# Banded attention into a feed-forward network: attention of two tiles at a time, the first block's cells partly in halves

## The chip, the cores and the metric

One core of one Trainium2 chip. The metric is the device time of one execution, in microseconds (us). Before the change the median of three runs is 890.47 us (890.44 to 892.8).

## What is computed

```python
# attention: 8 batches, 8 heads, 576 tokens, 64 values per head
scores = scale * np.matmul(q, k.transpose(0, 1, 3, 2))
mask = (rel >= 0) & (rel < 64)              # rel: query position minus key position
attn = softmax(np.where(mask, scores, -1e9))
x = heads_side_by_side(np.matmul(attn, v))   # 4608 tokens x 512
# network: w_in 512 x 2048, w_out 2048 x 512, alpha per hidden unit
h = x @ w_in
g = np.maximum(h, 0.0) + alpha * np.minimum(h, 0.0)
return (g @ w_out).astype(np.float32)
```

All is in 32-bit floats; the network's weights arrive as 64-bit floats and are converted on the core.

## The kernel before

Each matmul of the network is made of three: operands are split into a high and a low part (`xh`, `xl`, `wh`, `wl`), and high x high, high x low and low x high are added up.

**Attention** works on 36 tiles of 128 tokens, all eight heads of a tile together (`attention`, line 466). A tile's steps are: load q, k and v (SyncE's DMA queue); scores (`score`, line 404, TensorE, 32 matmuls of 64 x 64 weights into two banks of PSUM); masked minimum per head (`take_least`, 413, VectorE); exponential per head (`exponential`, 420, ScalarE); reciprocals of the sums (`invert`, 425 and 426, VectorE); scaling (`scale`, 430, GpSimd); turning the weights, either by VectorE's 16 transposes (440 and 442, the 23 tiles in `TURNED`) or by eight TensorE transposes (447) and copies out of PSUM (451); values (`value`, 463, TensorE, 48 matmuls); split into `xh` and `xl` (504 and 506).

**The first product** runs over 9 blocks of 4 tiles (512 tokens). A block has 16 cells (`cell`, line 513): 128 hidden units by 512 tokens, 12 matmuls (522) into one of four banks, then ScalarE's scaled copy (527), VectorE's max (528) and a store to memory, by way of four buffers. A cell of block n needs all four tiles of that block. Attention of block n + 1 stands between the cells of block n; that of tiles 0 to 3 comes ahead of the first cell. Tiles share one buffer of turned weights (`pt`).

**Weights** come in chunks (`chunk`, 302): ScalarE (318, 319), VectorE (323 or 321, 325), GpSimd (327), then the split (292, 288 or 289). The 16 chunks of `w_in` are converted while block 0 runs, those of `w_out` in blocks 1, 2, 4 and 5.

**The second product** (`second`, 561) follows, 36 units of seven steps of 12 matmuls (610), and is the same before and after.

**The order** is made by a planner (`Program.order`, line 73): each operation has an engine or a choice of two, a duration written into the program, the buffers that it reads and writes, and for TensorE a due time (`key`). The planner plays the engines, takes the ready operation that is due first, and writes down the order; each engine of the chip then runs its own list in that order, and waits for the others' results. From `ident` on until the fourth cell (`order`, line 662) gaps in TensorE's list are filled with dummy matmuls (`warm`, 274).

Of the kernel before, what the change touches and what calls it, by code (L numbers as in the profile page):

```python
# [41 lines left out]
class Op:  # L42
    def __init__(self, name, ways, key, earliest, service, at):
        self.name, self.ways, self.key, self.earliest, self.service, self.at = name, ways, key, earliest, service, at
        self.engine = next(iter(ways)) if len(ways) == 1 else None
        self.done = min(busy + LAGS[e] for e, (busy, _) in ways.items()) + (service + LANDING if "SP" in ways else 0.0)
        self.after, self.then, self.needs, self.due, self.begun = set(), [], 0, 0.0, False


class Program:  # L50
# [6 lines left out]
    def add(self, name, ways, reads=(), writes=(), key=None, earliest=0.0, service=0.0):  # L57
        o = Op(name, ways, key, earliest, service, len(self.ops))
# [14 lines left out]
    def order(self, fill):  # L73
# [7 lines left out]
        events, order, lanes, line, now = [], [], [], 0.0, 0.0  # L81
# [40 lines left out]
        while left:  # L122
            for e in ENGINES:
# [15 lines left out]
                o.busy = o.ways[e][0]  # L139
                order.append((now, o))  # L140
# [32 lines left out]
def banded_attention_then_prelu_ffn(  # L173
# [55 lines left out]
    turned = work.tile([P, 2, 2, 2, 2, W], F32, name="pt")  # L229
# [4 lines left out]
    ulps = work.tile([P, 512], I32, name="ulps")  # L234
# [4 lines left out]
    H_BANK, S_BANK, V_BANK = (0, 1, 2, 3), (4, 5), (6, 7)  # L239
# [33 lines left out]
    def warm():  # L273
        nc.tensor.matmul(banks[H_BANK[3]][:, :P], ident, ident, start=True, stop=True)  # L274
# [12 lines left out]
    def subtract_of(out, a, b):  # L287
        return {"DVE": (0.64, lambda: nc.vector.tensor_tensor(out=out, in0=a, in1=b, op=ALU.subtract)),
                "POOL": (1.29, lambda: nc.gpsimd.tensor_tensor(out=out, in0=a, in1=b, op=ALU.subtract))}

    def split(name, value, reads, hi, lo, hi_key, lo_key, earliest=0.0):
        p.add(name + ".h", {"ACT": (0.6, lambda: nc.scalar.copy(hi, value)), "POOL": (0.65, lambda: nc.gpsimd.tensor_copy(hi, value))},  # L292
              reads, [hi_key], earliest=earliest)
        p.add(name + ".l", subtract_of(lo, value, hi.bitcast(F32)), [*reads, hi_key], [lo_key], earliest=earliest)

    def two(name, to, a, b, op, reads, writes, earliest=0.0):
        p.add(name, {"DVE": (0.64, lambda: nc.vector.tensor_tensor(out=to, in0=a, in1=b, op=op)),
                     "POOL": (1.29, lambda: nc.gpsimd.tensor_tensor(out=to, in0=a, in1=b, op=op))}, reads, writes, earliest=earliest)
# [3 lines left out]
    def chunk(name, c, f, second, start=0.0):  # L302
        r = raw_at[0] % len(raws)
        raw_at[0] += 1
# [13 lines left out]
        add("rd." + name, "ACT", 0.57, lambda: nc.scalar.activation(ulps, low, AF.Copy, scale=2.0**-29), [k_raw], keys("e.ulps"), earliest=start)  # L318
# [3 lines left out]
        else:  # L322
            sh = lambda: nc.vector.tensor_scalar(out=bits, in0=bits, scalar1=3, scalar2=None, op0=ALU.logical_shift_left)  # L323
        add("sh." + name, "DVE", 0.6, sh, ["signs"] if second else [], [k_val], earliest=start)
        add("sg." + name, "DVE", 0.62, lambda: nc.vector.scalar_tensor_tensor(  # L325
            out=bits, in0=high, scalar=-2**31, in1=bits, op0=ALU.bitwise_and, op1=ALU.bitwise_xor), [k_raw], [k_val], earliest=start)
        p.add("jn." + name, {"POOL": (1.29, lambda: nc.gpsimd.tensor_tensor(out=bits, in0=bits, in1=ulps, op=ALU.add)),  # L327
                             "DVE": (0.66, lambda: nc.vector.tensor_tensor(out=bits, in0=bits, in1=ulps, op=ALU.add))},
              ["e.ulps"], [k_val, *both], earliest=start)
# [66 lines left out]
    def score(t):  # L396
        q = queries[t % 2].rearrange("p a (h w) -> p a h w", h=2)
        at = 2 * (t % KRING)
        for a in range(2):
            for h in range(2):  # L400
                for u in range(2):
                    for x in range(2):
                        r, us = slice(x * D, (x + 1) * D), slice(u * W, (u + 1) * W)
                        nc.tensor.matmul(bank_of(S_BANK[x])[us, 2 * a + h], q[r, a, h, us], kring[r, a, at + u:at + u + 2, h, :],  # L404
# [5 lines left out]
    def take_least(t, g):  # L410
# [3 lines left out]
            out=of_head(weights[t % 2], g), in0=bank_of(S_BANK[x])[:, e].rearrange("p (b k) -> p b k", b=2),  # L414
# [7 lines left out]
    def invert(t, u):  # L422
# [287 lines left out]
```

## Time and profile before

| | |
|---|---|
| profiled execution, its own time | 889.79 us |
| its span, first to last instruction | 888.1 us |
| TensorE (PE) busy | 872.5 us, 98%, 7910 matmuls |
| VectorE (DVE) busy | 698.0 us, 79% |
| ScalarE (ACT) busy | 458.7 us, 52% |
| GpSimd (POOL) busy | 205.0 us, 23% |
| granted clock of TensorE, mean | 0.998 |
| DMA, mean | 172 GB/s |
| chain that ended last, TensorE's share | 93% |

A busy share is a mean over stages with different limits, and TensorE's dummy matmuls count as busy. Matmuls overlap, so the length of one row is more than the time until the next starts; where the text counts TensorE's time it goes by the distance from start to start.

### The profile page before, as it was taken

The numbers are of one execution on the slowest core, as the hardware profiler recorded it, in microseconds if no ns is written. First come the engines' busy times: TensorE is split into PE (matmuls) and PEld (weight loads), VectorE is DVE, ScalarE is ACT, GpSimd is POOL, SyncE is SP. The second block draws the span as 40 slices with busy tenths as digits, with TensorE's granted clock in tenths as the row PEclk, the third lists the DMA queues.
The fourth block names the chain that finished last, engine by engine and source line by source line (L and its number), as shares of the span: only waits on it lengthen the run. The fifth ranks groups of instructions, "written<-read, shape, count | busy, mean of one in ns | idle before, by whom it ended". The sixth has DMA issues, their size and how long they took to land.

```text
span 888.1 us, 21316 instructions
## 1 busy us (share of the span) xinstructions
PE 872.5 (98%) x7910; PEld 781.7 (88%) x7910; DVE 698.0 (79%) x1835; ACT 458.7 (52%) x1176; POOL 205.0 (23%) x186
## 2 busy tenths in 40 slices
PE   7998899999999999999999999999999999999998
PEld 7986687888888888888888899999999999999997
DVE  3789889887797889779587457878888787878772
ACT  5887766565365674654553344444444444444440
POOL 4796645382017445311110000000000000000000
PEclk9999999999999999999999999999999999999999
DMA  6768654665366884744535995534444443535201
GB/s 188 237 206 257 196 170 158 214 198 184 114 199 232 270 270 161 260 156 138 179 114 178 354 323 178 159 108 150 119 140 131 136 143 108 154 107 156 72 25 48
DMA packets 121207, 152.91 MB, mean 172 GB/s; under 512 B 10512, under 2 KB 92432, under 8 KB 121104
## 3 DMA queue, kind: packets, MB, share of 16 engines
q1 hardware_dynamic: 121104, 151.56, 54.0%
q8 instruction: 62, 1.02, 0.5%
q14 instruction: 41, 0.34, 0.1%
HBM read 95.95 MB, written 55.57 MB: 171 GB/s over the span
## 4 chain that ended last, share of the span: by engine, by line
PE 93%; DVE 4%; issue 1%; POOL 1%; ACT 1%; POOLq 0%
PE bank L522 41%; PE bank L610 41%; PE bank L463 4%; PE bank L404 4%; PE bank L274 3%; PE bank L447 1%; DVE val L325 1%; DVE pt L440 1%; DVE val L323 1%; DVE pt L442 1%; ACT w L420 1%; DVE cell L528 1%; POOL w L430 0%; POOL val L327 0%; DVE xl L506 0%
## 5 line engine op out<-in xcount | busy, mean ns | idle before, releaser
L582 ACT CAST xh<-g 128x512 fp32r<-128x512 f32 x216 | 132.8, 621 | 155.0 <-PE bank L610 128.4
L583 DVE TENSOR_TENSOR xl<-g,xh 128x512 fp32r<-128x512 f32 x216 | 147.7, 689 | 38.5 <-ACT xh L582 35.1
L527 ACT ACTIVATE cell<-bank,alphas 128x512 f32<-128x512 f32 x144 | 98.9, 687 | 141.1 <-PE bank L522 132.8
L522 PE MATMUL bank<-xh,wh 128*128 128x512 f32 x576 | 161.4, 402 | 1.9 <-ACT wh L292 1.9
L610 PE MATMUL bank<-wh,xh 128*128 128x256 f32 x1008 | 161.3, 282 | 0.0
L610 PE MATMUL bank<-wl,xh 128*128 128x256 f32 x1008 | 161.3, 282 | 0.0
L610 PE MATMUL bank<-wh,xl 128*128 128x256 f32 x1008 | 161.3, 282 | 0.0
L522 PE MATMUL bank<-xl,wh 128*128 128x512 f32 x576 | 154.5, 390 | 0.0
L522 PE MATMUL bank<-xh,wl 128*128 128x512 f32 x576 | 154.1, 389 | 0.0
L528 DVE SCALAR_TENSOR_TENSOR cell<-bank,alphas,cell 128x512 f32<-128x512 f32 x144 | 105.2, 745 | 56.7 <-ACT cell L527 49.5
L610 PEld LDWEIGHTS bank<-wh,xh 128*128 128x128 f32 x1008 | 138.6, 191 | 0.1
L610 PEld LDWEIGHTS bank<-wl,xh 128*128 128x128 f32 x1008 | 138.2, 191 | 0.0
L610 PEld LDWEIGHTS bank<-wh,xl 128*128 128x128 f32 x1008 | 138.2, 191 | 0.0
L522 PEld LDWEIGHTS bank<-xl,wh 128*128 128x128 f32 x576 | 108.2, 188 | 23.5
L522 PEld LDWEIGHTS bank<-xh,wl 128*128 128x128 f32 x576 | 108.1, 188 | 22.8
L522 PEld LDWEIGHTS bank<-xh,wh 128*128 128x128 f32 x576 | 104.4, 189 | 26.4 <-issue 3.1
L420 ACT ACTIVATE w<-w,nm 128x128 f32<-128x128 f32 x288 | 111.9, 392 | 28.6 <-DVE nm L413 28.5
L430 POOL TENSOR_TENSOR w<-w,rc 128x512 f32<-128x512 f32 x72 | 78.2, 1087 | 185.9 <-DVE rc L426 174.6
L440 DVE STREAM_TRANSPOSE pt<-w 32x256 f32<-32x256 f32 x184 | 80.1, 436 | 5.7 <-POOL w L430 3.2
L578 DVE TENSOR_TENSOR g<-g,g 128x512 f32<-128x512 f32 x108 | 74.3, 688 | 2.1 <-DMA g<-g 0.6
L413 DVE CUSTOM_DVE_ANT_0 w<-bank,masks 128x128 f32<-128x128 f32 x288 | 63.9, 285 | 12.7 <-PE bank L404 11.2
L442 DVE STREAM_TRANSPOSE pt<-w 32x128 f32<-32x128 f32 x184 | 55.7, 303 | 2.9
(58 smaller groups left out, 763.8 us busy)
## 6 DMA issues: line engine op xcount, KB each, us to landing
g<-cell SPq DMA_DIRECT2D x144, 256.0 KB, 3.9
g<-g SPq DMA_DIRECT2D x144, 256.0 KB, 3.4
q<-qT SPq DMA_DIRECT2D x36, 256.0 KB, 4.3
out<-cell SPq DMA_DIRECT2D x36, 256.0 KB, 2.3
raw<-w_in SPq DMA_DIRECT2D x16, 512.0 KB, 4.7
raw<-w_out SPq DMA_DIRECT2D x16, 512.0 KB, 5.3
k<-kT SPq DMA_DIRECT2D x18, 384.0 KB, 4.2
v<-vN SPq DMA_DIRECT2D x18, 384.0 KB, 4.0
```

Of the source, the lines that this page charges most:

```text
L413: nc.vector.tensor_tensor_reduce(out=of_head(weights[t % 2], g), in0=bank_of(S_BANK[x])[:, e].rearrange("p (b k) -> p b k", b=2), in1=mask ...
L420: nc.scalar.activation(w, w, AF.Exp, scale=-1.0, bias=least[t % 2][:, g:g + 1], accum_out=sums[:, t % 2, g, 0:1])
L430: nc.gpsimd.tensor_tensor(out=w, in0=w, in1=rc.unsqueeze(1).unsqueeze(3).broadcast_to(list(w.shape)), op=ALU.mult)
L440: nc.vector.transpose(to, w[:, x, j])
L442: nc.vector.transpose(to[:, :, j ^ 1], w[:, x, j, :, j ^ 1])
L522: nc.tensor.matmul(h, w[KEPT + f][:, a * P:(a + 1) * P], v[:, a], start=k == a == 0, stop=k == 2 and a == NP - 1)
L527: add(f"sl.{n}.{f}", "ACT", 0.7, lambda: nc.scalar.activation(g, h, AF.Copy, scale=slope[:, f:f + 1]), ["signs", f"bank.{bank}"], [f"cell. ...
L528: add(f"la.{n}.{f}", "DVE", 0.72, lambda: nc.vector.scalar_tensor_tensor(out=g, in0=h, scalar=sign[:, f:f + 1], in1=g, op0=ALU.mult, op1=A ...
L578: add(name, "DVE", 0.64, lambda: nc.vector.tensor_tensor(out=to(), in0=a(), in1=b(), op=op), reads, writes)
L582: add(f"ys.{u}.{i}.h", "ACT", 0.6, lambda: nc.scalar.copy(x_hi[x], value()), ks, [f"xh.{x}"])
L583: add(f"ys.{u}.{i}.l", "DVE", 0.64, lambda: nc.vector.tensor_tensor(out=x_lo[x], in0=value(), in1=x_hi[x].bitcast(F32), op=ALU.subtract), ...
L610: nc.tensor.matmul(banks[bank][:, h * EH:(h + 1) * EH], part[x][:, j * HW + h * P:j * HW + (h + 1) * P], w[k][:, j * EH:(j + 1) * EH], sta ...
```

## The change

- Tiles 0 to 3 go one by one as before (`attend_one`), turned by TensorE in the banks of the scores. From tile 4 on two tiles go together (`attend_two`): one TensorE operation computes the scores of two tiles, and right behind it another the values of the two tiles before, so a stretch is scores, scores, values, values. The scores wait until the tiles before are ready for their values. Each tile of a pair has its own two banks of scores and its own buffer of turned weights.
- The cells get two banks in place of four.
- Each transpose of VectorE is an operation of its own for the planner (before, four were one). TensorE turns tiles 0 to 7, 9, 14, 19, 24, 29 and 34; VectorE the other 22.
- From tile 4 on all eight reciprocals of a tile are one operation. The splits into `xh` and `xl` take two tiles at a time.
- In block 0 the first five cells are computed in two halves of 256 tokens, the first half as soon as tiles 0 and 1 are there; the second halves stand between the whole cells 5 to 15.
- The fill of dummy matmuls ends with the second half cell (`h.0.1.0`).
- The low bits of the weights (`ulps`) get two buffers. Loads of v are issued behind the values before.
- The planner's durations and due times are others, and it plays GpSimd's operations and VectorE's ones with two inputs from SBUF (`paired`) one after the other.

The core of the diff:

```diff
-BEGIN = 30.0
-CELL = 3.22
+BEGIN = 16.0
+CELL = 3.25
 UNIT = 10.1
 STEP = 1.44
-TURNED = tuple(t for t in range(6, 36) if t % 4)
+SINGLE = 4
+HALVES = (18.0, 32.0)
+EARLY_HALVES = 5
+PACE = 3.8
+FIRST_TURNS = (34.0, 52.0, 68.0)
+PE_TURNED = (4, 5, 6, 7, *range(9, 36, 5))
...
                 o.busy = o.ways[e][0]
+                if e == "POOL" and o.busy or e == "DVE" and o.paired:
+                    o.busy += max(0.0, shared - now)
+                    shared = now + o.busy
...
-    turned = work.tile([P, 2, 2, 2, 2, W], F32, name="pt")
+    turned = [work.tile([P, 2, 2, 2, 2, W], F32, name=f"pt_{i}") for i in range(2)]
...
-    ulps = work.tile([P, 512], I32, name="ulps")
+    ulp_ring = [work.tile([P, 512], I32, name=f"ulps_{i}") for i in range(2)]
...
-    H_BANK, S_BANK, V_BANK = (0, 1, 2, 3), (4, 5), (6, 7)
+    H_BANK, S_BANK, V_BANK = (0, 1), ((2, 3), (4, 5)), (6, 7)
...
-        nc.tensor.matmul(banks[H_BANK[3]][:, :P], ident, ident, start=True, stop=True)
+        nc.tensor.matmul(banks[H_BANK[1]][:, :P], ident, ident, start=True, stop=True)
...
-    def transpose(t, u, i):
-        w = weights[t % 2]
+    def transpose(t, u, i, x, j):
+        pt = turned[t % 2]
         r = slice(u * W + i * 32, u * W + i * 32 + 32)
-        w = w[r].rearrange("p a b (h x) (j k) -> p x j a b h k", x=2, j=2)
-        for x in range(2):
-            for j in range(2):
-                to = turned[x * W + j * 32:x * W + j * 32 + 32, :, :, u, :, i * 32:i * 32 + 32].rearrange("p a h b q -> p a b h q")
-                if i == j:
-                    nc.vector.transpose(to, w[:, x, j])
-                else:
-                    nc.vector.transpose(to[:, :, j ^ 1], w[:, x, j, :, j ^ 1])
...
+    def turn(t, u, to):
         for b in range(2):
             for h in range(2):
-                nc.tensor.transpose(bank_of(V_BANK[u])[:, 2 * b + h],
+                nc.tensor.transpose(bank_of(to[u])[:, 2 * b + h],
...
+        for us in ([0], [1]) if t < SINGLE else ([0, 1],):
+            heads = slice(us[0] * NP, (us[-1] + 1) * NP)
+            add(f"rc.{t}.{us[0]}", "DVE", 0.3, lambda heads=heads: invert(t, heads), [f"e.sum.{t % 2}.{g}" for g in range(NH)[heads]], keys(*(f"e.rc.{t % 2}.{u}" for u in us)))
...
+        if not by_pe:
             for u in range(2):
                 for r in range(2):
-                    add(f"tr.{t}.{u}.{r}", "DVE", 1.4, lambda u=u, r=r: transpose(t, u, r), [f"{w}{g}" for g in range(NH)], keys(f"e.pt.{u}.{r}"))
-        else:
-            for u in range(2):
-                heads = range(u * NP, (u + 1) * NP)
-                add(f"tu.{t}.{u}", "PE", 0.44, lambda u=u: turn(t, u), [*(f"{w}{g}" for g in heads), "ident"], [v_banks[u]], key=begin + 0.5 * pace)
-                p.add(f"td.{t}.{u}", {"ACT": (0.57, lambda u=u: take_turned(t, u, nc.scalar.copy)), "DVE": (0.6, lambda u=u: take_turned(t, u, nc.vector.tensor_copy))},
-                      [v_banks[u]], keys(f"e.pt.{u}.0", f"e.pt.{u}.1"))
-        add(f"av.{t}", "PE", 0.95, lambda: value(t), [*vs, *(f"e.pt.{u}.{i}" for u in range(2) for i in range(2))], v_banks, key=begin + pace)
+                    for x in range(2):
+                        for j in range(2):
+                            add(f"tr.{t}.{u}.{r}.{x}.{j}", "DVE", 0.45 if r == j else 0.315, lambda u=u, r=r, x=x, j=j: transpose(t, u, r, x, j), w,
+                                keys(f"e.pt.{t % 2}.{u}.{r}.{x}.{j}"))
+
+    def turned_by_pe(t, to, key):
+        for u in range(2):
+            add(f"tu.{t}.{u}", "PE", 0.44, lambda u=u: turn(t, u, to), [*w_keys(t, u), "ident"], [f"bank.{to[u]}"], key=key)
+            p.add(f"td.{t}.{u}", {"ACT": (0.5, lambda u=u: take_turned(t, u, to, nc.scalar.copy)), "DVE": (0.6, lambda u=u: take_turned(t, u, to, nc.vector.tensor_copy))},
+                  [f"bank.{to[u]}"], keys(*pt_keys(t, [u])))
...
+    def x_parts(ts):
+        n, i = divmod(ts[0], BT)
...
+            from_ = bank_of(V_BANK[x]).rearrange("p (a i) q -> p a (i q)", a=2)[:, :, :len(ts) * P]
...
+    def attend_one(t, begin, pace):
+        loads(t, 0.0)
+        ring_load("v", t, 0.0)
+        add(f"s.{t}", "PE", 1.0, lambda: score(t), [f"e.q.{t % 2}", *ring_keys("k", t)], s_banks(t), key=begin)
+        softmax(t, True)
+        turned_by_pe(t, S_BANK[t % 2], begin + 0.5 * pace)
+        add(f"av.{t}", "PE", 1.0, lambda: value(t, 0), [*ring_keys("v", t), *pt_keys(t)], v_banks, key=begin + pace)
+        x_parts([t])
...
+    def values_of(ts, key):
+        def emit():
+            for i, t in enumerate(ts):
+                value(t, i)
+
+        add(f"av.{ts[0]}", "PE", 2.0, emit, [*(k for t in ts for k in ring_keys("v", t)), *(k for t in ts for k in pt_keys(t))], v_banks, key=key)
+        x_parts(ts)
+
+    def attend_two(ts, begin, before):
+
+        by_pe = [t for t in before if t in PE_TURNED]
+        for t in by_pe:
+            turned_by_pe(t, V_BANK, begin - 0.02)
+        if ts:
+            for t in ts:
+                loads(t, max(0.0, begin - 35.0))
+
+            def emit():
+                for t in ts:
+                    score(t)
+
+            wait = [k for t in before for k in (w_keys(t) if t in by_pe else pt_keys(t))]
+            add(f"s.{ts[0]}", "PE", 2.0, emit, [*(f"e.q.{t % 2}" for t in ts), *(k for t in ts for k in ring_keys("k", t)), *wait],
+                [k for t in ts for k in s_banks(t)], key=begin)
+        if before:
+            values_of(before, begin + 0.01)
+        for t in ts:
+            ring_load("v", t, max(0.0, begin - 20.0))
+        for t in ts:
+            softmax(t, t in PE_TURNED)
...
+    def cell(n, f, key, m=None):
...
+        at = counted[0] + (counted[0] % 2 if m is None else 0)
+        counted[0] = at + (2 if m is None else 1)
+        bank, c = H_BANK[at // 2 % 2], at // 2 % len(cells)
+        d, j, x = f % 8 // 2, f % 2, f // 8
+        parts = [0, 1] if m is None else [at % 2]
+        half = slice(0, 2 * HW) if m is None else slice(m * HW, (m + 1) * HW)
+        to = slice(parts[0] * HW, (parts[-1] + 1) * HW)
+        h, g = banks[bank][:, to], cells[c][:, to]
...
+                    nc.tensor.matmul(h, w[KEPT + f][:, a * P:(a + 1) * P], v[:, a, half], start=k == a == 0, stop=k == 2 and a == NP - 1, skip_group_check=True)
...
+        add(f"h.{name}", "PE", 12 * (0.2267 if m is None else 0.12), emit, [f"wh.{KEPT + f}", f"wl.{KEPT + f}", *needs], k_h, key=key)
+        add(f"sl.{name}", "ACT", 0.1 + 0.52 * part, lambda: nc.scalar.activation(g, h, AF.Copy, scale=slope[:, f:f + 1]), ["signs", *k_h], k_g)
...
-    for t in range(BT):
-        attention(t, 8.0 + 4.5 * t, 5.0)
+    for t in range(SINGLE):
+        attend_one(t, 6.0 + 4.5 * t, 5.0)
     for f in range(NF):
         convert_in(f)
+    pair = lambda j: [t for t in (2 * j, 2 * j + 1) if t < NT]
+    attend_two(pair(SINGLE // 2), FIRST_TURNS[0], [])
     for n in range(NB):
-        if n + 1 < NB:
-            for i in range(BT):
-                attention((n + 1) * BT + i, begin_of(n) + (i - 0.7) * 4 * CELL, 4 * CELL)
+        turns = [(2 * n + 3, 4), (2 * n + 4, 12)]
+        for j, f in turns:
+            if pair(j - 1):
+                attend_two(pair(j), begin_of(n) + (f - 0.5) * CELL if n else FIRST_TURNS[j - 2], pair(j - 1))
         for f in range(NF):
-            cell(n, f)
+            if n:
+                cell(n, f, begin_of(n) + f * CELL)
+        if n == 0:
+            for f in range(EARLY_HALVES):
+                cell(n, f, HALVES[0] + f * PACE, 0)
+            for f in range(NF - EARLY_HALVES):
+                if f < EARLY_HALVES:
+                    cell(n, f, HALVES[1] + f * PACE, 1)
+                cell(n, EARLY_HALVES + f, HALVES[1] + (f + 0.5) * PACE)
...
-    order = p.order(("ident", "h.0.3"))
+    order = p.order(("ident", "h.0.1.0"))
```

## Rows read from the trace of the kernel before

**Rows 1.** Windows: length, busy us (instructions) PE, PEld, DVE, ACT, POOL; clock, DMA, GB/s.
```profile
0.00:43.00 43.00, 38.36 (x629) 35.83 (x630) 23.03 (x138) 29.84 (x113) 24.26 (x32) 1.00 0.70 209
43.00:107.00 64.00, 57.39 (x500) 45.64 (x499) 55.66 (x163) 48.56 (x138) 47.26 (x39) 0.97 0.72 230
107.00:523.00 416.00, 416.00 (x3761) 339.64 (x3759) 329.98 (x1090) 225.04 (x674) 133.51 (x116) 1.00 0.61 199
```

**Rows 2.** The chain that ended last, in time: start, length, what.
```profile
523.16 360.65 PE bank L610 x3024
```

**Rows 3.** TensorE's timeline, first block's ends: start, length, engine, line, operation, count.
```profile
43.08 1.18 PE L522 MATMUL bank<-xh,wh 128*128 128x512 f32 x4
...
105.88 1.07 PE L522 MATMUL bank<-xh,wl 128*128 128x512 f32 x4
```

**Rows 4.** TensorE's waits: total, times, longest.
```profile
PE bank L463 <- DVE pt L440: 4.3, 2, 3.9
```

**Rows 5.** TensorE's timeline around stretches of attention.
```profile
124.48 1.13 PE L463 MATMUL bank<-pt,v 64*64 64x128 f32 x48
125.44 1.05 PE L404 MATMUL bank<-k,q 64*64 64x128 f32 x32
126.42 1.20 PE L522 MATMUL bank<-xh,wh 128*128 128x512 f32 x4
...
129.27 1.07 PE L522 MATMUL bank<-xh,wh 128*128 128x512 f32 x4
...
131.99 1.07 PE L522 MATMUL bank<-xh,wh 128*128 128x512 f32 x4
...
137.52 1.10 PE L404 MATMUL bank<-k,q 64*64 64x128 f32 x32
...
159.81 1.03 PE L447 MATMUL bank<-ident,w 128*128 128x128 f32 x8
160.59 1.17 PE L522 MATMUL bank<-xh,wh 128*128 128x512 f32 x4
...
245.34 1.10 PE L404 MATMUL bank<-k,q 64*64 64x128 f32 x32
246.26 1.08 PE L463 MATMUL bank<-pt,v 64*64 64x128 f32 x48
```

**Rows 6.** VectorE's timeline where tile 1's low parts are written.
```profile
26.62 0.75 DVE L506 TENSOR_TENSOR xl<-bank,xh 128x256 fp32r<-128x256 f32 x2
```

**Rows 7.** ScalarE's groups, 8 to 107 us: busy, mean ns, idle before.
```profile
L420 ACT ACTIVATE w<-w,nm 128x128 f32<-128x128 f32 x80 | 31.2, 395 | 10.0 <-DVE nm L413 10.0
```

**Rows 8.** VectorE's groups, 8 to 107 us.
```profile
L440 DVE STREAM_TRANSPOSE pt<-w 32x256 f32<-32x256 f32 x16 | 7.0, 435 | 0.6 <-POOL w L430 0.4
...
L442 DVE STREAM_TRANSPOSE pt<-w 32x128 f32<-32x128 f32 x16 | 4.8, 303 | 0.3
```

**Rows 9.** TensorE's and VectorE's timeline in the last block.
```profile
509.40 1.07 PE L522 MATMUL bank<-xh,wh 128*128 128x512 f32 x4
...
510.32 0.75 DVE L528 SCALAR_TENSOR_TENSOR cell<-bank,alphas,cell 128x512 f32<-128x512 f32 x1 [1.97 <-ACT cell L527]
```

**Rows 10.** The same two in the second block.
```profile
170.14 1.07 PE L522 MATMUL bank<-xh,wh 128*128 128x512 f32 x4
...
174.91 1.40 DVE L528 SCALAR_TENSOR_TENSOR cell<-bank,alphas,cell 128x512 f32<-128x512 f32 x2
```

**Rows 11.** The page's DMA issues: count, KB each, median us to landing.
```profile
k<-kT SPq DMA_DIRECT2D x18, 384.0 KB, 4.2
```

**Rows 12.** TensorE's timeline at its longest wait.
```profile
92.97 0.43 PE L463 MATMUL bank<-pt,v 64*64 64x128 f32 x2 [3.93 <-DVE pt L440]
93.76 1.98 PE L463 MATMUL bank<-pt,v 64*64 64x128 f32 x46 [0.36 <-DVE pt L440]
95.67 1.87 PE L522 MATMUL bank<-xh,wh 128*128 128x512 f32 x4
```

**Rows 13.** Windows, one stretch behind that wait.
```profile
95.00:96.00 1.00, 1.00 (x23) 0.88 (x16) 0.97 (x8) 0.25 (x2) 0.75 (x1) 0.50 0.00 0
```

More of the change, by code (lines that the diff above doesn't have):

```diff
@@ L80, in order @@
         until = dict.fromkeys(ENGINES, 0.0)
-        events, order, lanes, line, now = [], [], [], 0.0, 0.0
+        events, order, lanes, line, shared, now = [], [], [], 0.0, 0.0, 0.0
         left, filling = len(ops), False
@@ new lines, in ring_load, with loads, w_keys @@
+    def ring_load(kind, t, early):
+        new = slice(0 if t % KRING == 0 else 1, 3)
+        load = load_k if kind == "k" else load_v
+        add(f"{kind}.{t}", "SP", 0.5, lambda: load(t), (), keys(*ring_keys(kind, t)[new]), service=1.35 if t % KRING == 0 else 0.95, earliest=early)
+    def loads(t, early):
+        add(f"q.{t}", "SP", 0.5, lambda: load_q(t), (), keys(f"e.q.{t % 2}"), service=0.9, earliest=early)
+        ring_load("k", t, early)
+    def w_keys(t, u=None):
+        return [f"e.w.{t % 2}.{g}" for g in (range(NH) if u is None else range(u * NP, (u + 1) * NP))]
@@ L510, in begin_of @@
     def begin_of(n):
         return BEGIN + n * CELL * NF
-    def cell(n, f):
-        at = n * NF + f
-        bank, c, d, j, x = H_BANK[at % 4], at % 4, f % 8 // 2, f % 2, f // 8
-        h, g = banks[bank], cells[c]
+    counted = [0]
+    def cell(n, f, key, m=None):
[7 more added lines that the diff above has]
+        h, g = banks[bank][:, to], cells[c][:, to]
+        k_h, k_g = [f"bank.{bank}.{i}" for i in parts], [f"cell.{c}.{i}" for i in parts]
@@ L517, in cell @@
         xh, xl = xs[n % 2]
+        part = 1.0 if m is None else 0.5
         def emit():
@@ L521, in emit @@
                 for a in range(NP):
-                    nc.tensor.matmul(h, w[KEPT + f][:, a * P:(a + 1) * P], v[:, a], start=k == a == 0, stop=k == 2 and a == NP - 1)
-        slots = [4 * (n % 2) + a for a in range(NP)]
-        add(f"h.{n}.{f}", "PE", 12 * 0.2267, emit, [f"wh.{KEPT + f}", f"wl.{KEPT + f}", *(f"{part}.{i}" for i in slots for part in ("xh", "xl"))],
-            [f"bank.{bank}"], key=begin_of(n) + f * CELL)
-        add(f"sl.{n}.{f}", "ACT", 0.7, lambda: nc.scalar.activation(g, h, AF.Copy, scale=slope[:, f:f + 1]), ["signs", f"bank.{bank}"], [f"cell.{c}.0"])
@@ new lines, in cell @@
+        add(f"la.{name}", "DVE", 0.06 + 0.6 * part, lambda: nc.vector.scalar_tensor_tensor(
+            out=g, in0=h, scalar=sign[:, f:f + 1], in1=g, op0=ALU.mult, op1=ALU.max), ["signs", *k_h], k_g)
+        far_to = hidden[n][d].rearrange("p (m x) j t -> p x j m t", x=2)[:, x, j]
+        if m is None:
+            store = lambda: nc.sync.dma_start(far_to, g.rearrange("p (m t) -> p m t", m=2))
+        else:
+            store = lambda: nc.sync.dma_start(far_to[:, m], g)
+        add(f"gs.{name}", "SP", 0.5, store, k_g, [f"far.g.{n}.{d}.{2 * y + x}.{j}" for y in (range(2) if m is None else [m])], service=0.9 * part)
```

142 lines of the change are left out of this document (69 added, 73 removed).

## The prediction

> **What bounds the kernel now.** I read the busy table by stage first, then TensorE's waits, then TensorE's timeline where they fall. The windows [rows 1] cut the run at the first cell of the first product (43 us), the end of its first block of tokens (107 us) and the start of the second product (523 us). From 107 to 523 us TensorE is busy in 416.00 of 416 us; after that the chain of waits runs through one unbroken piece of 3024 matmuls, 360.65 us [rows 2]. There only less TensorE work can save time. Before 107 us a busy TensorE misleads: most of it up to 43.08 us, where the first cell starts [rows 3], is attention of four tiles and dummy matmuls of the fill. Between 43 and 107 us it stands still for 6.6 us, and the longest wait is 3.9 us for the transposes of VectorE [rows 4]. So there are two places to gain: what TensorE spends beside its cells after 107 us, and how late the first block ends. That is at 105.88 + 0.91 = 106.8 us, where the last four matmuls of its last cell end [rows 3].
>
> The sum is made against the profiled execution, 889.8 us (span 888.1 and 1.7 around it). The median of the runs shown, 890.47, lies 0.7 above; my number is on the scale of the profiled one, and the range covers that.
>
> **Pairs, after the first block.** A cell is 131.99 - 129.27 = 2.72 us. From 126.42 to 137.52 lie four cells, 11.10 us, 0.22 more than 4 x 2.72: that is what a stretch of small matmuls costs the cells at its two edges. A stretch "values then scores" takes 126.42 - 124.48 = 1.94, so 2.16 with its edges [rows 5]. From 106.8 to 523.0 us, 128 cells make 348.2 of 416.2 us, and attention has 68.0. Counted in the timeline, these are 17 stretches of two pieces (36.7 us), 20 of one piece, and six tiles turned by TensorE at 160.59 - 159.81 = 0.78 and some 0.1 at the edges (5.3). The 20 lone pieces are left with 26.0, 1.30 each, edges included.
> The change needs for the same 26 scores and 28 values 13 stretches of four pieces and a last one of two values. Values ahead of scores take 125.44 - 124.48 = 0.96, scores ahead of values 246.26 - 245.34 = 0.92, scores ahead of a cell 0.98 [rows 5]. Scores ahead of scores are in no row; I take 0.92, its nearest neighbour, with 0.85 to 0.98 as ends. One stretch: 0.92 + 0.92 + 0.96 + 0.98 + 0.22 = 4.0 us. 13 x 4.0 + 2.2 + 5.3 (again six turned tiles) = 59.5. The gain is 68.0 - 59.5 = 8.5; I take 8, between 7 and 9.5.
>
> **The first block.** TensorE's own list until its end, in the changed order: 16 cells 43.5; five of them as halves cost 24 x 360.65 / 3024 = 2.86 instead of 2.72 each [rows 2], +0.7; four single tiles, each 2 x 1.30 + 0.9, 14.0; scores of tiles 4 and 5, 2.2; two stretches of four, 8.0; tiles 4 to 7 turned, 3.6. Sum 72.0. A half cell needs tiles 0 and 1 alone; VectorE wrote the low part of tile 1 at 26.62 to 27.4 us [rows 6], so that is when it could start. Ahead of it TensorE has three scores, two values and two turned tiles, 8.3 of the 27.4 us: 19.1 are lost to the chain of the softmax. With no other wait the block ends at 72.0 + 19.1 = 91 us.
> The helpers hardly allow that. ScalarE was busy 29.84 + 48.56 = 78.4 us up to 107 [rows 1]; 16 of its 80 exponentials (0.39 us each, 6.3 in all [rows 7]) belong to tiles 8 and 9, which the next block needs; two more tiles turned by TensorE add four copies out of PSUM and the halves five more reads, about +3, an estimate that takes them as eight instructions of 0.39. That is 75 us from about 10 us on: 85 at no idle time, 93 at a tenth idle, against a fifth now. VectorE loses the transposes of tiles 6 and 7, 7.0 + 4.8 = 11.8 us [rows 8], which stood in front of the longest wait; they go to TensorE. I put the end at 95: the 91, and 4 for weights that come late. The gain is 106.8 - 95 = 11.8. Its ends are 16 (no such wait) and 4 (end at 103, if the conversion sets the pace as now).
>
> **Two banks for the cells in place of four.** This is the wait that the change adds. Undisturbed, a cell's bank is free 1.67 us after its end: the cell ends at 509.40, VectorE's max runs from 510.32 to 511.07 [rows 9]. With two banks the cell after the next starts 2.72 us after that end, so 1.0 us may be lost to whatever ScalarE and VectorE have in hand. With four banks nobody had to hurry: the cell that ends at 170.14 is read by a max that begins at 174.91, behind sixteen transposes [rows 10]. The plan now must cut in, and can, since each transpose is an operation of its own, of 0.30 to 0.44 us [rows 8]. A late max holds all cells and the next stretch behind it on TensorE, and the loss is paid in full. I take 3 us in all, 0.02 per cell; ends 0 and 9.
>
> **Nothing for the rest.** Loads of k and q may now wait for the stretch before: some 25 us (eight cells and a stretch) ahead of their use against 4.2 us of landing [rows 11]; without that cover a stretch would start 4 us late. On SyncE's queue they stand ahead of stores of cells, and four cell buffers cover some 11 us. One load for two tiles' values and merged casts save VectorE and ScalarE tenths, off the path. The second buffers for turned weights and low bits only loosen waits. The planner's new durations and its shared turn of GpSimd and VectorE move the order alone, and their worth is in the waits above. The second product is the same instructions in the same order and stays at its length.
>
> **The sum.** 889.8 - 8 - 11.8 + 3 = 873.0 us.
>
> **Rivals.**
> - *A, nothing waits:* the first block ends at 91 and two banks cost nothing: 889.8 - 8 - 16 = 866. For it: TensorE has not one wait in 416 us now [rows 1], from a plan with coarser times. Against it: ScalarE would need almost no idle time.
> - *B, the first block is paced by the helpers:* it ends at 103 as weights and softmax come no sooner. 889.8 - 8 - 4 + 3 = 881. For it: VectorE is busy 55.66 of 64 us between 43 and 107 us [rows 1]. Against it: 11.8 us of that go.
> - *C, the clock:* after its wait of 3.93 us TensorE runs at a granted clock of 0.50, its 1.2 GHz level, and the piece from 93.76 to 95.67 lasts 1.91 instead of about 1.0, the next four matmuls are slow as well: some 1.6 us lost [rows 12, 13]. The fill of dummy matmuls that covered all gaps up to 43 us now ends with the second half cell, near 28 us, so later gaps are bare. Three such gaps cost 4.8: 873 + 5 = 878. It speaks against this that the waits summed above are 4 us in all, in pieces.
> - *D, two banks decide, and the kernel gets slower:* if the max ends late by a mean of 0.2 us per cell, 144 cells lose 28.8: 889.8 - 8 - 11.8 + 28.8 = 899. It decides from 19.8 / 144 = 0.14 us per cell. For it: VectorE is 79% busy from 107 to 523 us and works in long runs [rows 1, 10]. Against it: a queue that is planned for it needs to place one max every 2.72 us, and a transpose in hand costs 0.44 of the 1.0 us.
>
> On C, the Trainium skill ("TensorE: Matmul & The Clock Gate", Part 1) says that the slow clock is the default state and that only activity releases it, which speaks against a shorter fill. By that rule the sum would be the 878 of C instead of 873. The trace agrees for its one long wait (0.50 [rows 13]).
>
> **Chances.** The forecast 0.48, A 0.16, B 0.16, C 0.10, D 0.10. The predicted time is the forecast's, 873. The range 863 to 884 holds A, B and C with a few us of spread (the ends of the pairs and of the waits) and leaves out D and the tails. A measurement of this kernel can tell about 0.3%, 2.7 us. Faster by more than that: the forecast, A, C and nearly all of B, 0.88; within it: the rest of B and a mild D, 0.04; slower: D, 0.08.
>
> **What would show it.** Right: 15 stretches of 64 score and 96 value matmuls, about 3.8 us each, no TensorE idle between them and the second product 416 - 5 = 411 us after the end of the first block; first cells with 256 columns near 27 us; the first block's end near 95 us. Wrong: waits of first product matmuls for VectorE's cell (D, every one on the bank); waits for ScalarE's or GpSimd's weights between 40 and 100 us and an end past 100 (B); a granted clock of 0.50 in windows before 95 us (C); a stretch that waits for transposes, which would be a new wait that I priced at nothing.

## The result and the profile after

The changed kernel takes 879.89 us (median of four runs, 878.87 to 883.31) against 890.72; the ratio is 0.988, with an interval of 0.9849 to 0.9911. The forecast was 873.0, its range 863 to 884. The profiled execution took 878.87 us, 10.9 less than the one before. The three stretches of [rows 1], cut in the changed kernel where they now end: first cell, end of the first block, start of the second product (length, then busy us and instructions of PE, PEld, DVE, ACT, POOL; clock, DMA share, GB/s).

```profile
0.00:27.00 27.00, 22.37 (x342) 20.91 (x343) 14.30 (x80) 17.33 (x66) 12.61 (x22) 1.00 0.72 202
27.00:101.00 74.00, 66.69 (x791) 57.96 (x790) 57.21 (x185) 64.09 (x190) 54.72 (x46) 0.98 0.79 246
101.00:512.00 411.00, 407.75 (x3757) 341.26 (x3756) 331.05 (x1037) 213.15 (x627) 134.60 (x119) 1.00 0.62 203
```

After the first block TensorE is no longer busy all the time: 407.75 of 411 us. The events that cut these stretches, from TensorE's timeline (start, length, what, and idle time ahead in brackets) and, last, from the chain of waits:

```profile
27.03 0.71 PE L599 MATMUL bank<-xh,wh 128*128 128x256 f32 x4
...
100.58 1.07 PE L599 MATMUL bank<-xh,wh 128*128 128x512 f32 x4
...
512.52 0.64 PE L691 MATMUL bank<-wh,xh 128*128 128x256 f32 x4
...
512.68 360.65 PE bank L691 x3024
```

The first half cell starts at 27.03 (forecast 27.4, before 43.08 [rows 3]). The first block ends at 100.58, where the next block's first cell begins (forecast 95, before 106.8). From there to the second product it is 512.52 - 100.58 = 411.9 us (forecast 411, before 416.2). What follows lasts 877.2 - 512.5 = 364.7 us, before 888.1 - 523.0 = 365.1. So 6.2 + 4.3 + 0.4 = 10.9 us came from these three places.

TensorE's waits in the changed kernel (total, times, longest), to be laid beside [rows 4]:

```profile
PE bank L599 <- DVE cell L606: 4.9, 4, 2.6
PE bank L282 <- POOL ident L266: 4.6, 1, 4.6
PE bank L599 <- ACT wh L300: 1.7, 1, 1.7
PE bank L469 <- issue: 1.2, 2, 0.7
PE bank L469 <- ACT pt L457: 1.1, 1, 1.1
PE bank L599 <- POOL wl L297: 0.9, 1, 0.9
PE bank L453 <- POOL w L438: 0.8, 1, 0.8
```

The long wait for transposes is gone. In its place stands the wait that the change added: a cell of the first product that may not enter its bank until VectorE's max (L606) has read it.

### The profile page after: what moved, and what is told of

Read it like the earlier page. It is cut to its first block, busy times and chain, and to the rows that moved or that the text cites. A ratio compares the mean times of both kernels' runs of the same rounds, so it can differ in the third digit from the quotient of the medians.

```text
span 877.2 us, 21173 instructions
## 1 busy us (share of the span) xinstructions
PE 858.1 (98%) x7912; PEld 781.1 (89%) x7912; DVE 690.9 (79%) x1745; ACT 449.9 (51%) x1135; POOL 201.9 (23%) x185
## 4 chain that ended last, share of the span: by engine, by line
PE 88%; DVE 4%; ACT 3%; DMA 2%; issue 1%; POOL 1%; POOLq 0%; DVEq 0%; SPq 0%; ACTq 0%
PE bank L691 41%; PE bank L599 39%; PE bank L469 3%; PE bank L413 3%; DMA raw<-w_in 2%; ACT w L429 2%; DVE cell L606 1%; PE bank L282 1%; PE bank L453 1%; DVE pt L446 1%; DVE val L334 1%; DVE pt L448 0%; ACT val L328 0%; DVE val L332 0%; POOL val L306 0%
## 5 line engine op out<-in xcount | busy, mean ns | idle before, releaser
L605 ACT ACTIVATE cell<-bank,alphas 128x512 f32<-128x512 f32 (+1 forms) x149 | 100.2, 673 | 168.2 <-PE bank L599 155.1
L599 PE MATMUL bank<-xh,wh 128*128 128x512 f32 (+1 forms) x596 | 159.0, 388 | 6.6 <-DVE cell L606 4.9
L606 DVE SCALAR_TENSOR_TENSOR cell<-bank,alphas,cell 128x512 f32<-128x512 f32 (+1 forms) x149 | 108.3, 730 | 66.5 <-ACT cell L605 55.3
L599 PE MATMUL bank<-xh,wl 128*128 128x512 f32 (+1 forms) x596 | 155.6, 383 | 0.9 <-POOL wl L297 0.9
L599 PE MATMUL bank<-xl,wh 128*128 128x512 f32 (+1 forms) x596 | 155.6, 383 | 0.0
L599 PEld LDWEIGHTS bank<-xh,wh 128*128 128x128 f32 x596 | 107.9, 188 | 30.9 <-DVE cell L606 7.6
L599 PEld LDWEIGHTS bank<-xh,wl 128*128 128x128 f32 x596 | 110.3, 189 | 22.8 <-POOL wl L297 1.1
L599 PEld LDWEIGHTS bank<-xl,wh 128*128 128x128 f32 x596 | 110.1, 188 | 22.2
L438 POOL TENSOR_TENSOR w<-w,rc 128x512 f32<-128x512 f32 x72 | 76.9, 1086 | 128.8 <-DVE rc L434 110.7
L446 DVE STREAM_TRANSPOSE pt<-w 32x256 f32<-32x256 f32 x176 | 76.7, 436 | 4.8 <-POOL w L438 1.5
L422 DVE CUSTOM_DVE_ANT_0 w<-bank,masks 128x128 f32<-128x128 f32 x288 | 63.5, 284 | 12.4 <-PE bank L413 10.9
L336 POOL TENSOR_TENSOR val<-val,ulps 128x512 int32<-128x512 int32 x30 | 40.3, 1349 | 78.0 <-DVE val L334 71.3
```

Of the source, the lines that this page charges most:

```text
L336: p.add("jn." + name, {"POOL": (1.27, lambda: nc.gpsimd.tensor_tensor(out=bits, in0=bits, in1=ulps, op=ALU.add)), "DVE": (0.62, lambda: nc ...
L422: nc.vector.tensor_tensor_reduce(out=of_head(weights[t % 2], g), in0=bank_of(S_BANK[t % 2][x])[:, e].rearrange("p (b k) -> p b k", b=2), i ...
L438: nc.gpsimd.tensor_tensor(out=w, in0=w, in1=rc.unsqueeze(1).unsqueeze(3).broadcast_to(list(w.shape)), op=ALU.mult)
L446: nc.vector.transpose(to, w[:, x, j])
L599: nc.tensor.matmul(h, w[KEPT + f][:, a * P:(a + 1) * P], v[:, a, half], start=k == a == 0, stop=k == 2 and a == NP - 1, skip_group_check=True)
L605: add(f"sl.{name}", "ACT", 0.1 + 0.52 * part, lambda: nc.scalar.activation(g, h, AF.Copy, scale=slope[:, f:f + 1]), ["signs", *k_h], k_g)
```

## Experiments on the two banks

Theory: two banks cost little in themselves, and the plan decides. Rival: they cost 0.2 us per cell wherever they are used. In the runs that put two banks into the kernel before, the dummy matmuls move into the second bank, and their fill ends with the second cell in place of the fourth.

**Two banks alone, in the kernel before.**

```
-    H_BANK, S_BANK, V_BANK = (0, 1, 2, 3), (4, 5), (6, 7)
+    H_BANK, S_BANK, V_BANK = (0, 1), (4, 5), (6, 7)
-        bank, c, d, j, x = H_BANK[at % 4], at % 4, ...
+        bank, c, d, j, x = H_BANK[at % 2], at % 4, ...
```

> The kernel before, with two banks for the cells in place of four and nothing else of the change. Theory (two banks cost little where the plan knows of them): 0.02 to 0.06 us per cell, 3 to 9 us in all, 894 to 900 us, and the waits of the first product's matmuls stand on VectorE's max. Rival (two banks decide): 0.2 us per cell or more, 29 us, about 919 us. If the time stays within 2 us of 890.7, two banks cost nothing even with the coarse transposes of the plan before.

915.37 us, ratio 1.0281 (1.0264 to 1.0298): 25 us slower, the rival's size. But the waits are not the rival's (waits, then TensorE's timeline at one stretch):

```profile
PE bank L463 <- DVE pt L440: 14.7, 28, 2.9
PE bank L522 <- DVE cell L528: 2.9, 2, 2.3
...
214.08 1.10 PE L404 MATMUL bank<-k,q 64*64 64x128 f32 x32
215.53 0.43 PE L463 MATMUL bank<-pt,v 64*64 64x128 f32 x2 [0.34 <-DVE pt L440]
216.32 1.12 PE L463 MATMUL bank<-pt,v 64*64 64x128 f32 x46 [0.36 <-DVE pt L440]
217.37 1.20 PE L522 MATMUL bank<-xh,wh 128*128 128x512 f32 x4
```

Cells wait for a bank only twice. Instead the values of a tile stand right behind the next tile's scores and wait for VectorE's transposes, so a stretch of scores and values lasts 217.37 - 214.08 = 3.29 us where it took 1.93 before. There are 15 such stretches, before there were 7. Added up from the timeline, all stretches of attention after the first block last 79.0 us against 58.6: 20 of the 28 us by which the two profiled executions differ (918.08 against 889.79); 3.9 us more lie ahead of the end of the first block (110.7). The price is real, its place is another.

**The same with the changed kernel's planned times** (four transposes at 1.53 us in place of 1.4, an exponential at 0.39 and so on): is the list wrong because the plan took the transposes to be shorter than they are?

```
-    add(f"tr.{t}.{u}.{r}", "DVE", 1.4, ...
+    add(f"tr.{t}.{u}.{r}", "DVE", 1.53, ...
```

> The kernel before with two banks for the cells, as in e1_before_two_banks, and with the changed plan's durations (four transposes 1.53 us in place of 1.4, a masked minimum 0.215 in place of 0.29, and the others). Theory (the 25 us of two banks came from values that wait for transposes which the plan had too short, and that four banks hid): most of it goes, 893 to 900 us. Rival (the banks themselves hold TensorE): 908 to 916 us.

947.6 us, ratio 1.0612 (1.0584 to 1.0641). Both expectations missed: the better times made it 32 us worse, with 29.4 us of waits for transposes in 31 pieces. Part of it is the clock: its mean is 0.978 over a span of 945.7 us, against 0.992 over 916.4 us with two banks alone, which by one minus the clock times the span is up to 21 us lost against up to 7. That theory fell.

**Two banks, each transpose a step of its own.** One part of the change, alone, in the kernel before.

```
-    add(f"tr.{t}.{u}.{r}", "DVE", 1.4, lambda: transpose(t, u, r), ...
+    for x in range(2):
+        for j in range(2):
+            add(f"tr.{t}.{u}.{r}.{x}.{j}", "DVE", 0.35, lambda: transpose(t, u, r, x, j), ...
```

> The kernel before with two banks for the cells (915.4 us), and each of the four 32x32 transposes that one step held made a step of its own, planned at 0.35 us (the four together as before, 1.4 us), so that a max of a cell need not wait behind four of them. Theory 'distance' (two banks cost 25 us because the values of a tile follow its scores by one tile, 13 us, so that the transposes are due at once and take TensorE's next work with them): the size of a transpose step matters little, 910 to 920 us, with some 12 to 16 us of waits of the values for transposes still there. Rival 'size of the step' (a max stuck behind four transposes keeps a bank closed 1.5 us longer): most of the 25 us comes back, 893 to 903 us, and the waits of the values fall under 5 us.

914.21 us, ratio 1.0261 (1.0244 to 1.0278), 1.2 us less than with coarse steps, and the two intervals overlap. TensorE still waits 15.0 us for transposes. The step's size is not the cause there.

**Two banks, values one tile later.**

```
-    add(f"av.{t}", "PE", 0.95, ..., key=begin + pace)
+    add(f"av.{t}", "PE", 0.95, ..., key=begin + (pace if t < BT else 2 * pace))
-                attention((n + 1) * BT + i, begin_of(n) + (i - 0.7) * 4 * CELL, 4 * CELL)
+                attention((n + 1) * BT + i, max(21.0, begin_of(n) + (i - 1.7) * 4 * CELL), 4 * CELL)
```

> The kernel before with two banks for the cells (915.4 us), the values of each tile from the fifth on due one tile later (beside the scores of the tile after the next), with two buffers for the transposed weights and the tiles' begins moved one tile earlier, so that the values still end before their block. Transposes stay four in a step. Theory 'distance': with a whole tile more between scores and values the transposes are no longer urgent and most of the 25 us comes back: 892 to 904 us, the waits of values for transposes under 4 us in all. Rival 'size of the step': nothing that matters has changed, 908 to 920 us.

897.71 us, ratio 1.0072 (1.0049 to 1.0096): 17.7 of the 25 us come back. In its trace no wait for transposes is left and the banks cost 0.4 us (its last line among TensorE's waits, then where the second block's first cell starts, then the chain's last piece):

```profile
PE bank L522 <- DVE cell L528: 0.4, 2, 0.2
...
110.69 1.07 PE L522 MATMUL bank<-xh,wh 128*128 128x512 f32 x4
...
528.38 360.65 PE bank L610 x3024
```

Its first block ends at 110.69, as with two banks alone (110.71) and 3.9 us later than with four. From there to the second product it is 417.5 us, against 441.0 with two banks alone and 416.2 with four. So nearly the whole price of two banks after the first block hung on how soon the values follow their scores, together with the second buffer of turned weights that the edit brings.

**The changed kernel with four transposes in a step.**

```
-                    for x in range(2):
-                        for j in range(2):
-                            add(f"tr.{t}.{u}.{r}.{x}.{j}", "DVE", 0.45 if r == j else 0.315, ...
+                    add(f"tr.{t}.{u}.{r}", "DVE", 1.53, four, w, ...
```

> The changed kernel with four transposes in one step again (planned at 1.53 us), everything else as changed: two banks, pairs, values a whole pair behind their scores. Theory 'distance': the pairs already make the transposes patient, so coarse steps cost little, 878 to 885 us. Rival 'size of the step': the changed kernel's small price for two banks comes from the fine steps, and coarse ones bring the old price back: 890 to 905 us.

891.89 us, ratio 1.0011 (0.9998 to 1.0023): 12 us slower than the change, and the theory missed. Here the cells do wait for their banks, as in the rival of the prediction:

```profile
PE bank L602 <- DVE cell L609: 10.5, 18, 2.6
```

In 12 of the 18 waits the max stands right behind a run of VectorE's transposes and comes too late by 0.3 to 0.7 us. So in the changed kernel both parts are needed: the pairs take the urgency out of the transposes, the small steps let the max in. Coarse steps need not cost this much: with the values one tile later, above, they are as coarse and the banks cost 0.4 us. Why they cost more with the pairs is not shown.

## Experiments on the first block

**No halves.** `EARLY_HALVES = 5` becomes 0.

> The changed kernel without half cells: the first block's 16 cells are whole. Theory (TensorE's own list and its waits set the end of the first block): the first cell starts near 38 us in place of 27, some 7 us of cell work lies behind it, less 0.7 for the dearer halves: 6 us slower, 886 us. Rival (weights and softmax pace the first block): the same end of the block within 1 us, 880 us.

887.54 us, ratio 0.997 (0.9955 to 0.9984): 7.6 us more than the change. The first cell starts at 37.75, the block ends at 108.13. Not all of that is the halves' own. The list now puts a stretch of pairs (tile 9 turned, scores of 10 and 11, values of 8 and 9) ahead of the block's last three cells. Yet from the block's end on, with that stretch of some 4.7 us gone, it takes 413.1 us to the second product, against 411.9 in the change. There VectorE's max is late twice by 2.21 us, behind subtractions of VectorE that last 2.92 and 3.77 us, and the clock falls to 0.50 after the first wait. How much of the 7.6 us the halves alone save is not shown.

**Tiles 6 and 7 turned by VectorE again.** `PE_TURNED = (4, 5, 6, 7, ...)` loses 6 and 7.

> The changed kernel with tiles 6 and 7 turned by VectorE, as before, in place of TensorE. Theory (11.8 us of transposes in the first block stood in front of its end): VectorE gets 12.2 us more, TensorE 1.8 less; the first block ends 3 to 8 us later, 883 to 888 us. Rival (VectorE has the room): 878 to 880 us.

884.4 us, ratio 0.9916 (0.9898 to 0.9934), 4.5 slower than the change, as expected. The block ends at 105.67, behind a wait of 3.1 us for weights; waits for VectorE's max are 7.8 us in all, against 4.9.

**Three buffers for raw weights.** `raws` gets a third tile.

> The changed kernel with three buffers for the raw weights in place of two. Theory (bank waits and the slow clock behind them make the miss): at most 1 to 2 us earlier, 878 to 880 us, the wait of 2.6 us on VectorE's max stays. Rival (the loads of raw weights, 5 to 7 us each into two buffers, pace the first block): the waits for weights go and the block ends 3 to 5 us earlier, 875 to 877 us.

878.15 us (877.57 to 879.45), ratio 0.9867 (0.9852 to 0.9881): 1.7 less than the change, in the theory's range, though the runs of the two touch. The block ends at 98.37, 2.2 us sooner, less than the rival asked. The longest wait for a bank is 1.5 us in place of 2.65, which the theory had as staying, and the clock stays at 1.00. From there to the second product it takes 414.7 us in place of 411.9, so the profiled execution (879.45) is no shorter than that of the change (878.87).

**The reads of a cell's bank planned first** (keys for ScalarE's copy and VectorE's max two and 1.3 us ahead of the cell's).

```
-        add(f"sl.{name}", "ACT", ..., ["signs", *k_h], k_g)
+        add(f"sl.{name}", "ACT", ..., ["signs", *k_h], k_g, key=key - 2.0)
```

> The changed kernel with ScalarE's and VectorE's reads of a cell due two seconds' worth of the plan's microseconds earlier (2.0 us before the cell's own due time), so that they go ahead of softmax and weights. Theory (bank waits and the slow clock behind them make the miss): the 4.9 us of waits on VectorE's max go, and with them 1 to 2 us of slow clock; some comes back as later softmax: 875 to 877 us. Rival (the helpers have no time to spare, the wait only moves to the weights or the softmax): 879 to 882 us.

881.76 us, ratio 0.9908 (0.9893 to 0.9923): the theory missed, and the time is the rival's. The banks still cost 4.2 us, the waits for weights (`wh`, `wl`) grew from 2.6 to 3.1, and the block ended at 103.05. That the helpers' time was short and not ill ordered fits this; it is not shown apart from other changes of the order.

**Three raw buffers and a third buffer for low words.**

> The changed kernel with three buffers for the raw weights (878.2 us alone) and, for the sixteen conversions of the first block, a third buffer for the low words, which takes the place of a buffer that is idle then. Theory 'loads and their buffers set the pace of the conversions': the first block ends a microsecond or two sooner than with three raw buffers alone (98.4), 875 to 878 us. Rival 'the two banks and the helpers' own work set the pace': no gain over three raw buffers alone, 877.5 to 880 us.

881.38 us, ratio 0.9893 (0.9848 to 0.9939): no gain that can be told. The block ends at 97.92, 0.45 us sooner than with three raw buffers alone. Its four executions lie in two groups, 877.48 and 877.71 against 885.04 and 885.13, and the profiled one is of the second. One step in it is about as much too long as the 7.5 us between the groups (VectorE's, GpSimd's and TensorE's timelines):

```profile
119.34 7.93 DVE L296 TENSOR_TENSOR wl<-val,wh 128x512 fp32r<-128x512 f32 x1
127.19 0.74 DVE L607 SCALAR_TENSOR_TENSOR cell<-bank,alphas,cell 128x512 f32<-128x512 f32 x1
...
117.80 4.03 POOL L439 TENSOR_TENSOR w<-w,rc 128x512 f32<-128x512 f32 x4
121.80 1.25 POOL L306 TENSOR_TENSOR val<-val 128x512 f32<-128x512 f32 x1
123.02 2.48 POOL L297 TENSOR_TENSOR wl<-val,wh 128x512 fp32r<-128x512 f32 x2
125.46 1.25 POOL L297 TENSOR_TENSOR wl<-delta,wh 128x512 fp32r<-128x512 f32 x1
...
127.98 2.08 PE L600 MATMUL bank<-xh,wh 128*128 128x512 f32 x4 [6.01 <-DVE cell L607]
```

A subtraction of VectorE of the size that takes 0.69 us at L665 lasted 7.93 us. It began while GpSimd was at work and ended 0.6 us after the last of GpSimd's next six steps, which ran without a break to 126.71; the max behind it came late, and TensorE waited 6.01 us. That this step is as short as its like in the two shorter executions fits, but they have no trace. Elsewhere the longest step of VectorE was a like subtraction of 3.77 us, in the run without halves, which also ended 0.55 us after the last of the GpSimd steps that ran beside it (209.54 and 208.99); in all other profiled runs none lasted over 1.9 us.

## Experiments on the planner's times

**No shared turn of VectorE and GpSimd in the plan**, the traced times kept.

```
-                if e == "POOL" and o.busy or e == "DVE" and o.paired:
+                if False:
```

> The changed kernel, planned without the shared turn of GpSimd and VectorE; durations as changed. Theory (the conversions of weights are where both meet, so the plan is too early there): waits of TensorE for the max and for transposes in blocks 0, 1, 2, 4 and 5, 2 to 6 us, 882 to 886 us. Rival (the model of the shared turn is worth nothing): 879 to 881 us.

883.17 us (881.07 to 885.3), ratio 0.9902 (0.9877 to 0.9927): 3.3 more than the change, as expected, though the two intervals overlap. TensorE waits 7.1 us for the max, nine times; of the expected waits for transposes there are none.

**Neither that nor the new times.**

> The changed kernel, planned with the durations of the kernel before (a transpose 0.35 us whatever its shape) and without the shared turn of GpSimd and VectorE. Theory (with two banks the plan's times must be true): TensorE waits for transposes ahead of values in each of the some 12 stretches with them and for VectorE's max: 10 us or more slower, 889 to 900 us. Rival (the structure alone makes the gain): 880 to 884 us.

879.87 us, ratio 0.9868 (0.9847 to 0.9889), the time of the change itself; the theory missed by 9 us. The block ends at 100.45. So the traced times and the shared turn together bring nothing in this structure. With the traced times alone all four executions (881.07 to 885.3) are longer than the four here (879.21 to 880.67); that the shared turn takes this back is likely, but the overlap above leaves it open.

## Why the prediction came out as it did

On the scale of the profiled execution the forecast missed by 5.9 us, 878.9 against 873.0, and 5.6 of them are the end of the first block: 100.6 in place of 95.

**The pairs: right.** After the first block, thirteen stretches of two scores and two values stand where they were forecast. The two of the first block do not: there the list puts cells between the scores and the values, so it is thirteen in place of fifteen. One lasts 168.50 - 164.79 = 3.71 us, as forecast without edges (0.92 + 0.92 + 0.96 + 0.98 = 3.78):

```profile
164.79 1.98 PE L413 MATMUL bank<-k,q 64*64 64x128 f32 x64
166.58 1.98 PE L469 MATMUL bank<-pt,v 64*64 64x128 f32 x96
168.50 1.19 PE L599 MATMUL bank<-xh,wh 128*128 128x512 f32 x4
```

The gain between block end and second product is 4.3 us. Three stretches are longer than their like, by 0.76, 0.92 and 0.21 us, for a halt inside the values that the profile puts to "issue" in the first two; no row of before had it, and I priced it at nothing:

```profile
249.68 0.34 PE L469 MATMUL bank<-pt,v 64*64 64x64 f32 x7 [0.50 <-issue]
...
276.30 0.35 PE L469 MATMUL bank<-pt,v 64*64 64x64 f32 x9 [0.70 <-issue]
```

Add these 1.9 us to the 4.3, and the 2.0 us of bank waits after 100.6 us (0.65 at 150.96, 1.36 at 175.60), and the pairs gave 8.2, where I took 8 between 7 and 9.5. Only a third of that is shorter attention. Before, attention after the first block stands in 44 pieces that last 58.6 us; now it stands in 15 that last 57.7, or 55.8 without the halts. The rest is the edges of the cells beside these pieces: without attention, 128 cells of 2.72 us and the 2.0 us of bank waits, 9.4 us were left before and 4.0 are now. No run takes the pairs alone. The nearest, two banks with the values of single tiles one tile later, needs 417.5 us for this part, 5.6 more than the change.

**Two banks: mechanism right, size wrong. This is the mis-sized term.** I took 3 us, spread over 144 cells. The rows have 2.0 after the block, 2.9 in it, and the clock on top. The longest wait and what follows it (TensorE's timeline; windows of 1 us, the column before the last two is the granted clock):

```profile
56.55 0.74 PE L599 MATMUL bank<-xh,wh 128*128 128x256 f32 x4 [2.65 <-DVE cell L606]
57.13 0.95 PE L599 MATMUL bank<-xl,wh 128*128 128x256 f32 x4
57.88 1.05 PE L599 MATMUL bank<-xh,wl 128*128 128x256 f32 x4
...
57.00:58.00 1.00, 1.00 (x8) 1.00 (x7) 1.00 (x11) 1.00 (x5) 1.00 (x2) 0.63 0.97 239
58.00:59.00 1.00, 1.00 (x7) 1.00 (x7) 0.18 (x2) 0.81 (x3) 1.00 (x2) 0.50 0.75 203
59.00:60.00 1.00, 1.00 (x6) 1.00 (x5) 0.28 (x3) 1.00 (x3) 1.00 (x1) 0.50 1.10 345
60.00:61.00 1.00, 1.00 (x6) 0.93 (x5) 1.00 (x8) 0.81 (x3) 0.03 (x1) 0.67 0.97 327
```

The clock lost in these four windows is 0.37 + 0.50 + 0.50 + 0.33 = 1.7 us. With it the two banks took 2.0 + 2.9 + 1.7 = 6.6 us, inside the ends 0 to 9 but more than twice the value taken. My undisturbed 1.67 us [rows 9] hid who else wants the two readers in the first block (ScalarE's and VectorE's timelines):

```profile
53.89 1.07 ACT L457 COPY pt<-bank 128x512 f32<-128x512 f32 x2
54.35 0.47 DVE L606 SCALAR_TENSOR_TENSOR cell<-bank,alphas,cell 128x256 f32<-128x256 f32 x1
54.75 1.36 DVE L334 SCALAR_TENSOR_TENSOR val<-raw,val 128x512 int32<-128x512 int32 x1
54.86 0.47 ACT L605 ACTIVATE cell<-bank,alphas 128x256 f32<-128x256 f32 x1
56.03 0.47 DVE L606 SCALAR_TENSOR_TENSOR cell<-bank,alphas,cell 128x256 f32<-128x256 f32 x1
```

ScalarE's read at 54.86 stands behind two copies of turned weights, and VectorE's max at 56.03 behind a conversion of 1.36 us. But these two read the other half of the bank. By the order that the planner writes, the half cell that waits is `h.0.2.1`, in the first half of its bank; that half was read for the last time by the max at 54.35 (of `h.0.1.1`), done at 54.82. The reads at 54.86 and 56.03 are of `h.0.0.1`, which TensorE had finished at 39.2 in the second half of the same bank. TensorE starts 0.05 us after the last of them. So the plan counts the halves of a bank as two buffers, and the kernel waits for the reads of both. In the run with neither the shared turn nor the new times the first cell to use its half (`h.0.3.0`) waits in the same way, for ScalarE's read of the other:

```profile
44.24 0.71 PE L599 MATMUL bank<-xh,wh 128*128 128x256 f32 x4 [1.44 <-ACT cell L605]
```

Some 1.7 of the 2.65 us (54.82 to 56.50) are therefore a price of the half cells in shared banks, for which the sum had no term. With the reads planned first, where `h.0.0.1` is read early, `h.0.2.1` still waits 1.80 us for its own half.

Nor does the lower clock follow from the wait alone. With four transposes in a step TensorE's list is the same here and the same half cell waits as long, but the clock stays at 1.00 and the block ends at 99.71 (TensorE's timeline, then windows with all engines):

```profile
56.54 0.74 PE L602 MATMUL bank<-xh,wh 128*128 128x256 f32 x4 [2.63 <-DVE cell L609]
...
58.00:59.00 1.00, 1.00 (x12) 1.00 (x11) 0.46 (x5) 1.00 (x3) 1.00 (x2) 1.00 0.82 214
59.00:60.00 1.00, 1.00 (x7) 0.83 (x6) 1.00 (x7) 1.00 (x3) 1.00 (x1) 1.00 1.01 350
```

So the 1.7 us of clock are in part chance: they belong to the execution profiled.

**The first block: right but for that.** Take the 2.9 and 1.7 from 100.6 and 96.0 is left, against 95 forecast. This is a sum of rows, not a run: where a run took a wait away by priority, another came. The 106.8 of before needs a word: by the planner's order the next block's first cell (`h.1.0`) ran ahead of the first block's last (`h.0.15`) there, so at 106.8 sixteen cells were done, and the block's own last one ended 2.7 us later. The sum counts cells, and its terms stay as they are. Its other waits, 1.7 + 0.9 + 1.1 + 0.8 = 4.5 us, are the 4 that I took, for the copies as well as for weights.

The terms then give 889.8 - 8.2 - (106.8 - 96.0) + 6.6 + 1.9 - 0.4 = 878.9, the profiled time. They must, since they are read from the same trace: this is a share-out, and no test of it.

**The rivals.** A did not come: the banks were not free. B's time was nearly met, nearer than the forecast's: its 881 is 1.1 from the median of 879.9, the forecast's 873 is 6.9. The run with tiles 6 and 7 on VectorE (4.5 us) shows that the helpers' work bears on the block's end; the run without halves speaks for TensorE's own list, as far as its 7.6 us are the halves'. The block does end past 100, but B's condition, want of weights, is 2.6 us of waits in the rows. C came once, for 1.7 us, and not three times. D's size is real in the kernel before (25 us, 0.17 per cell), though TensorE waits there for transposes and only twice for a bank. D's mechanism is real in the changed kernel with coarse steps (12 us), where I gave it 0.10 on the argument that a transpose is an operation of its own and can be cut into. That argument holds with the pairs and not without them: in the old structure small steps gave back 1.2 us of 25, no more than the runs can tell.

## What to carry to other kernels

A price per item read from an undisturbed stretch ("free after 1.67 us, needed after 2.72") is a floor; the busiest stretch, with the same engines in other work, sets what is paid. A plan that counts two halves of a bank as two buffers is right only if the kernel waits for them one by one; here it did not. Taking buffers from a list that a planner makes can cost far from the buffers: look where the list puts the work that may now run, and give that work slack before making its steps smaller. Test parts of a change alone and with the part that they lean on; here the small steps brought back 1.2 us at most without the pairs and 12 us with them.

## What the runs showed of the hardware

- A VectorE step can stand behind a whole run of GpSimd steps: 7.93 us in place of 0.69, ending 0.6 us after the one under way and six more were done. The Trainium skill ("SBUF — State Buffer", section "SBUF: two separate sides") says that the two share a port pair as an exclusive lock, which an instruction of VectorE with two inputs in SBUF also needs against one of GpSimd that reads SBUF; whichever starts first holds it for the whole instruction, and the other blocks fully. The trace agrees that such a subtraction is held up, and here it was held for a row of instructions and not for one.
- Waits of TensorE of nearly the same length went with a lower clock and without. The one of 2.65 us in the changed kernel was followed by a granted clock of 0.50, the 1.2 GHz level, and so was one of 2.21 us in the run without halves. The one of 2.63 us with four transposes in a step was not, nor one of 2.52 us in the run with neither the shared turn nor the new times, nor the one of 1.70 us at 43.93 in the changed kernel (the window from 42 to 48 us has 1.00). What decides is not shown.
- A half cell waits for the reads of the other half of its bank: some 1.7 of 2.65 us at 56.55 in the changed kernel, 1.44 us at 44.24 in the run with neither the shared turn nor the new times. Whether the chip asks for that or only the way in which this kernel orders its waits is not shown.
- TensorE halts for 0.5 and 0.7 us inside two stretches of values with no releaser in the profile ("issue"). What holds it is not shown.
